# Batch 0's first attention in pieces, and batch 1's last values over another queue: an attention and feed-forward kernel on one Trainium2 core

## The chip, the core and the metric

The kernel runs on one core of one Trainium2 chip. The core has a matrix engine (TensorE, PE in the profile; PEld is its loading of weights), a vector engine (VectorE, DVE), an engine for activation functions (ScalarE, ACT), a general one (GpSimd, POOL) and one that mostly starts transfers (SyncE, SP). They run their own instruction streams in order and wait for each other by semaphores. Transfers (DMAs) are started from the queues of SP, ACT and POOL and share 16 DMA engines. PE writes its results to PSUM, the other data lies in SBUF.

The metric is the device time of the whole program in microseconds (us). Of the kernel before, three runs are given: 307.8, 309.38 and 309.56 us, median 309.38.

## The reference

There are 8 batches, 8 heads, 576 tokens and a head dimension of 64. Two attentions are added, and the sum goes through a feed-forward layer:

```python
q_d, k_d, v_d = means over 4 neighbouring tokens          # 144 tokens
out_d = softmax(q_d @ k_d.T / 8) @ v_d                    # "down"
out_up = repeat(out_d, 4)                                 # back to 576 tokens
mask = abs(pos[:, None] - pos[None, :]) < 4               # 7 neighbours
out_local = softmax(where(mask, q @ k.T / 8, -1e9)) @ v   # "local"
x = (out_up + out_local) as (8 * 576 tokens, 512)
h = x @ w_in                                              # 512 x 2048
out = (h * sigmoid(1.702 * h)) @ w_out                    # 2048 x 512
```

Inputs and outputs are 32-bit floats; the matmuls of the kernel take bf16.

## The kernel before, in words

All tokens together (4608) are worked through in 9 groups of 512. For a group `g`, `mm1` (L753) multiplies 16 chunks of `w_in` with the transposed attention result `xT` into PSUM (L738), ACT applies the activation (L749) into `gT`, and `mm2` (L770) multiplies with `w_out` (L808) and stores (`store`, L783). While group `g` is computed, the attention of batch `g + 1` is interleaved with its matmuls: the list `POS` or `POS_G` gives the places n (0 to 15 in `mm1`, 16 and up are the matmuls of `mm2`) at which the scores, the exponentials, the products with the values and the normalisations are issued. All engines follow an order that is written out by hand: each runs its instructions in program order.

Batch 0 has nothing to hide behind. It is done ahead of the loop, in the lines L847 to L938, and this is where most of the change lies. Its steps are these.

- **Loads.** `load_qk` (L192) and `load_vb` (L212) start transfers from POOL's queue that convert to bf16. A chunk of values `vb[:, i]`, i from 0 to 4, has 128 rows (two overlapping halves of 64 tokens) and comes in two transfers of 64 KB. Chunks 0 to 3 of batch 0 come this way; chunk 4 comes unconverted by `load_v` (L196), over SP's and ACT's queues, and ACT converts it (`prep_v`, L323). A transfer from POOL's queue waits until the eighth transfer before it has landed: they take turns on eight semaphores.
- **Scores.** `scores` and `scores_d` (L394, L411) give the local and the down scores of four heads, `exp_local` and `exp_down` (L477, L483) take their exponentials on ACT into `es` and `ed`.
- **Values of the down attention.** `prep_vd_pe` (L351) sums 4 neighbouring value rows by matmuls with the selection matrices `psel` (L362): part kc 0 needs chunks 0 and 1, kc 1 needs 1, 2 and 3, kc 2 needs 3 and 4. ACT copies the sums to `vd` (L371).
- **Products.** For a pair of heads `hp`, `av_local0` (L493, matmuls at L499) gives the local result into PSUM tile `o[hp]`, columns 0 to 259 from chunks 0 to 3 (two blocks of 65 columns from chunks 0 and 1, two from 2 and 3) and the rest from chunk 4; `av_down0` (L507, matmuls at L513 and L522) the down result. The tiles are `PA[0]`, `PA[1]`, `PA[2]` and `PA[0]` again for the four pairs; the scores use the same tiles before.
- **Norms.** `normalise0` (L537) divides by the sums on DVE: a reciprocal (L541), the product for the down part (L544) and for the local part (L549). Part "a" is columns 0 to 3 of seven, part "b" the rest.
- **Turning.** `turned` (L917) transposes and adds both results by matmuls with an identity (`transp_sum`, L564 and L575), and ACT copies them to `xT` (`copy_x`, L587 and L591).
- **First half of group 0.** `part` (L907) issues matmuls of `mm1` (L738) as soon as one pair's `xT` is there, in between the turning of the pairs.
- **Fillers.** `warm` (L603) issues matmuls on constants whose result nobody reads.

In the loop, for g = 0, POOL's queue starts the loads of batch 1's values, of `w_out` (four transfers of chunks 0 to 3, 4 to 7, 8 to 11, 12 and 13, 14 and 15; the first two are started ahead of the loop), and batch 2's q and k. `mm2` of group 0 takes chunks 0 to 7 of `w_out` first. At n = `VDP_0` batch 1's values are summed with `prep_vd_pe`; `by_head_dim` at places 42 and 56 gives batch 1's products and norms (`av_t`, L681, and `normalise_t`, L690 to L710).

Of the kernel before, what the change touches and what calls it, by code (L numbers as in the profile page):

```python
# [19 lines left out]
def kernel(  # L20
# [175 lines left out]
    def load_v(b, gate=None, chunks=range(5), queues=(nc.sync, nc.sync)):  # L196
        t = ldp.tile([128, 5, H, D], FP32, name="vf", tag="vf")
        vf[b] = t
        if gate is not None:
            gate(t[0:1, 0, 0, 0:1])  # L200
        for i in chunks:
            for par in range(2):
                queues[par].dma_start(
                    out=t[64 * par : 64 * par + 64, i],
                    in_=bass.AP(
                        tensor=v.tensor,
                        offset=v[b, 0].offset + (114 * i + KSTART[par]) * D,
                        ap=[[D, 64], [S * D, H], [1, D]],
                    ),
                )  # L210

    def load_vb(b, i):  # L212
        for par in range(2):
# [137 lines left out]
    def prep_vd_pe(b, pv, kcs=range(3), between=None):  # L351
        n = HP
        vb, vd = vbs[b % 2], vds[b % 2]
        for kc, iis in ((0, (0, 1)), (1, (1, 2, 3)), (2, (3, 4))):
            if kc not in kcs:
                continue
            c0 = 256 * (kc - kcs[0])
            if between and kc == 1:
                between()
            for i in iis:  # L360
                for j in range(2):
                    nc.tensor.matmul(  # L362
                        pv[64 * j : 64 * j + 64, c0 : c0 + D * n],
                        lhsT=psel[:, PSEL.index((i, kc)), :],
                        rhs=sub(
                            vb[:, i], 65 * (2 * j if b else j), (4 * 65, NQ), (65 * (1 if b else 2), 2), (1, D)
                        ),
                        start=(i == iis[0]), stop=(i == iis[-1]),
                        tile_position=(0, 64 * j),
                    )  # L370
        nc.scalar.copy(  # L371
            out=vd[:, kcs[0] : kcs[-1] + 1, :, 0:D],
            in_=pv[:, 0 : 256 * len(kcs)].rearrange(
                "p (k h d) -> p k h d", k=len(kcs), h=HP
            ),
        )
# [160 lines left out]
    def normalise0(o, y, u, parts="ab"):  # L537
        yl, yd, rc = y
        ov = o[:, :, 0:455].rearrange("p x (c e) -> p x c e", e=65)
        c0, c1 = {"a": (0, 4), "b": (4, 7), "ab": (0, 7)}[parts]  # L540
# [229 lines left out]
    def mm2(g, gT, steps):  # L770
# [29 lines left out]
        for t, ffc, run in order:  # L800
# [13 lines left out]
            if ffc == n_ffc - 1:  # L814
                store(t, ops[t], 0, d_model, nc.scalar, nc.sync, part.get(t))
# [23 lines left out]
    POS_G = {0: [16, 18, 29, 42, 56, 65], 1: [13, 16, 35, 44, 58, 65]}  # L839
    VDP_0 = 34  # L840
# [18 lines left out]
    warm(5, 256)  # L859
# [21 lines left out]
    load_w_out(4)  # L881
# [7 lines left out]
    warm(1, z=wf)  # L889
    prep_vd_pe(0, PM[0], range(0, 2))  # L890
    for hp in range(2):
        av_local0(hp, o[hp], range(5))
        normalise0(o[hp], y[hp], hp % 2, "a")
    prep_vd_pe(0, PM[1], range(2, 3))
    exp_down(1, scores_d(0, 1, PA[2]))
    nc.scalar.preload_act_table_set("silu_and_others")
    for hp in range(2):
        if hp == 1:
            warm(1, t=PM[0])
        av_down0(hp, o[hp])  # L900
        normalise0(o[hp], y[hp], hp % 2, "b")

# [9 lines left out]
    def av_whole0(hp):  # L912
        av_local0(hp, o[hp], range(5))
        av_down0(hp, o[hp])
        normalise0(o[hp], y[hp], hp % 2)

# [5 lines left out]
    av_whole0(2)  # L922
    warm(1, t=PM[0])
    turned(0, None)
    av_whole0(3)
# [14 lines left out]
    for g in range(n_groups):  # L940
        b = g + 1
        if g == 0:
            load_vb(1, 0)
# [6 lines left out]
            load_vb(1, 4)  # L950
# [57 lines left out]
        if b < B:  # L1008
# [3 lines left out]
            if g == 0:  # L1012
                steps.setdefault(VDP_0, []).append(lambda: prep_vd_pe(1, flat(PA[1])))
# [43 lines left out]
```

## Time and profile before

| what | value |
|---|---|
| median of the three runs shown | 309.38 us (307.8 to 309.56) |
| the profiled execution's own time | 308.58 us |
| its span, first to last instruction | 306.8 us, so 1.8 us lie around it |
| PE busy | 298.0 us, 97% of the span |
| ACT, DVE, POOL busy | 212.9, 187.1 and 178.9 us |
| PE busy between 0 and 13.5, 13.5 and 19, 19 and 24, 24 and 38.6 us | 10.56, 4.62, 3.56, 14.53 us |
| DMA traffic over the span | HBM read 44.83 MB, written 9.44 MB |

The profile shows one execution on the chip. Its page gives busy times, the chain of work that ended last and groups of instructions by line; the trace behind it can be asked for a timeline (instructions in order of time, merged where they are alike), for waits (who waited for whom) and for transfers. In a timeline a row has its start and length in us, then engine, line, operation, what it writes and reads, and in brackets the idle time ahead of it with what ended it. "issue" there is idle time that nothing in the profile explains. In the rows of DMA queues, q0 is POOL's, q1 SP's and ACT's, and the "instruction" queues bring the engines' own programs.

### The profile page before, as it was taken

To read this page: it belongs to the slowest core of one execution; us is meant where nothing else is said; L and a number is where in the kernel's file an instruction comes from. 1 tells how busy PE (TensorE), PEld (TensorE's weight loads), DVE (VectorE), ACT (ScalarE), POOL (GpSimd) and SP (SyncE) were. 2 spreads that over 40 slices of the span, in tenths; PEclk is the share of its full clock that TensorE was granted. 3 is DMA by queue.
4 is the path that set the end of the run, shared out by engine and by line. 5 is a ranking of instruction groups with operands and counts; after the bars stand their busy time and mean duration, and the time that the engine had idled before them with its cause. 6 is when DMAs were issued, how large, how long until landed. Compare 5 with 4: busy or idle time off the path is not lost.

```text
span 306.8 us, 8494 instructions
## 1 busy us (share of the span) xinstructions
PE 298.0 (97%) x3551; PEld 147.8 (48%) x3551; DVE 187.1 (61%) x354; ACT 212.9 (69%) x351; POOL 178.9 (58%) x217
## 2 busy tenths in 40 slices
PE   7879999999999999999999999999999999999995
PEld 3455455444554455445544554455444544444444
DVE  6865523966999689886897689777975430000000
ACT  5545887867887788668966896689769876226511
POOL 8855792599698968976797669845983300000000
PEclk9999999999999999999999999999999999999999
DMA  7999999999899969826973598425101110010012
GB/s 147 152 203 209 173 132 213 177 221 215 177 230 188 188 133 226 219 46 113 232 211 66 88 218 232 84 77 150 72 0 37 36 71 0 34 71 34 0 68 71
DMA packets 64662, 40.01 MB, mean 130 GB/s; under 512 B 44656, under 2 KB 56048, under 8 KB 64624
## 3 DMA queue, kind: packets, MB, share of 16 engines
q0 software_dynamic: 18352, 14.81, 35.8%
q1 hardware_dynamic: 45600, 24.46, 32.3%
q8 instruction: 28, 0.46, 0.6%
q10 hardware_dynamic: 672, 0.20, 0.3%
q14 instruction: 10, 0.08, 0.1%
HBM read 44.83 MB, written 9.44 MB: 177 GB/s over the span
## 4 chain that ended last, share of the span: by engine, by line
PE 93%; DMA 4%; issue 1%; POOL 1%; DVE 0%; ACT 0%; POOLq 0%; DVEq 0%
PE pm L808 40%; PE pm L738 36%; PE pa L681 5%; PE pa L738 5%; DMA qb<-in_q_dram 2%; DMA vb<-in_v_dram 2%; PE pa L449 2%; PE pm L824 1%; PE pa L458 1%; PE pa L394 1%; PE pa L411 0%; POOL kb L183 0%; PE pa L513 0%; PE pa L362 0%; PE pa L499 0%
## 5 line engine op out<-in xcount | busy, mean ns | idle before, releaser
L808 PE MATMUL pm<-w_out_bf,gT 128*128 128x512 bf16 x560 | 126.2, 379 | 0.0
L738 PE MATMUL pm<-xT,w_in_bf 128*128 128x512 bf16 x512 | 119.2, 379 | 0.3 <-ACT xT L591 0.3
L749 ACT ACTIVATE gT<-pm 128x512 bf16<-128x512 f32 x128 | 76.3, 598 | 42.7 <-PE pm L738 42.7
L738 PEld LDWEIGHTS <-w_in_bf 128*128 128x128 bf16 x576 | 55.6, 98 | 67.2 <-issue 0.6
L808 PEld LDWEIGHTS <-gT 128*128 128x128 bf16 x560 | 52.9, 98 | 62.2 <-issue 0.4
L699 DVE TENSOR_TENSOR xT<-pa,r 128x300 bf16<-128x300 f32 (+3 forms) x112 | 28.0, 303 | 18.6 <-ACT r L694 17.8
L787 ACT ACTIVATE osb<-pm 128x512 f32<-128x512 f32 (+2 forms) x37 | 21.5, 580 | 24.1 <-PE pm L808 21.3
L708 POOL TENSOR_TENSOR xT<-xT,ydt 128x576 bf16<-128x576 bf16 x14 | 16.2, 1173 | 31.1 <-DVE xT L699 31.1
L789 DVE TENSOR_SCALAR osb<-pm 128x128 f32<-128x128 f32 x1 | 0.3, 292 | 55.5 <-ACT osb L787 55.5
L491 DVE TENSOR_TENSOR es<-es,mask 128x600 bf16<-128x600 bf16 x28 | 19.0, 708 | 21.2 <-ACT es L477 20.9
L693 ACT ACTIVATE r<-pa 128x504 f32<-128x504 f32 (+1 forms) x42 | 24.0, 571 | 8.4 <-PE pa L681 8.4
L694 ACT ACTIVATE r<-r 128x504 f32<-128x504 f32 (+1 forms) x42 | 25.9, 616 | 1.3
L339 POOL TENSOR_TENSOR v<-v 112x512 f32<-112x512 f32 x18 | 23.5, 1306 | 0.4
L277 DVE TENSOR_REDUCE kT<-kT 32x576 bf16<-32x576 bf16 x22 | 17.5, 795 | 8.7 <-POOL odd L272 8.3
L261 DVE STREAM_TRANSPOSE kT<-kb 128x576 f32<-128x576 f32 x16 | 20.0, 1252 | 3.4 <-DMA kb<-in_k_dram 3.1
L477 ACT ACTIVATE es<-pa 128x600 bf16<-128x600 f32 x32 | 19.7, 668 | 3.4 <-PE pa L394 3.2
L261 DVE STREAM_TRANSPOSE qT<-qb 128x576 f32<-128x576 f32 x16 | 19.8, 1238 | 0.7 <-DMA qb<-in_q_dram 0.3
L738 PE MATMUL pa<-xT,w_in_bf 128*128 128x512 bf16 x64 | 20.0, 379 | 0.0
L315 POOL TENSOR_TENSOR pq<-qT 128x576 f32<-128x576 bf16 x14 | 16.0, 1145 | 6.8 <-DVE qT L277 6.6
L277 DVE TENSOR_REDUCE kT<-odd 32x576 bf16<-32x576 bf16 x22 | 17.5, 795 | 0.7
L277 DVE TENSOR_REDUCE qT<-qT 32x576 bf16<-32x576 bf16 x22 | 17.5, 795 | 0.7
L277 DVE TENSOR_REDUCE qT<-odd 32x576 bf16<-32x576 bf16 x22 | 17.4, 791 | 0.7
(107 smaller groups left out, 344.2 us busy)
## 6 DMA issues: line engine op xcount, KB each, us to landing
out_dram<-osb SPq DMA_DIRECT2D x35, 256.0 KB, 3.2
vf<-in_v_dram SPq DMA_DIRECT2D x61, 128.0 KB, 4.3
v<-in_v_dram SPq DMA_DIRECT2D x72, 96.0 KB, 4.2
kb<-in_k_dram POOLq DMA_DIRECT2D x16, 288.0 KB, 7.1
qb<-in_q_dram POOLq DMA_DIRECT2D x16, 288.0 KB, 9.4
w_in_bf<-in_moe_w_in_dram POOLq DMA_DIRECT2D x4, 512.0 KB, 7.5
w_out_bf<-in_moe_w_out_dram POOLq DMA_DIRECT2D x3, 512.0 KB, 15.6
vb<-in_v_dram POOLq DMA_DIRECT2D x18, 64.0 KB, 6.3
```

The lines of the kernel that those rows point to most:

```text
L261: nc.vector.transpose(out=t32.rearrange("p (i c) -> p c i", c=18), in_=store[b, qd].bitcast(FP32).rearrange("p (c d) -> p c d", c=18),)
L277: nc.vector.tensor_reduce(out=dst, in_=src[:, :, None], axis=mybir.AxisListType.X, op=ALU.add)
L339: eng.tensor_tensor(out=t1[0:112], in0=x[:, :, 0:2, :], in1=x[:, :, 2:4, :], op=ALU.add)
L477: nc.scalar.activation(out=es[2 * qd + u][:, :, 0:300], in_=sp[u][:, :, 0:300], func=AF.Exp, scale=inv_sqrt_d,)
L491: nc.vector.tensor_tensor(out=ev, in0=ev, in1=mask, op=ALU.mult)
L693: nc.scalar.activation(out=r, in_=den, func=AF.Ln)
L694: nc.scalar.activation(out=r, in_=r, func=AF.Exp, scale=-1.0)
L699: nc.vector.tensor_tensor(out=sub(x[u], t0 + at, (114, n), (1, c)), in0=sub(src, c0, (60, n), (1, c)), in1=sub(rc, c0, (60, n), (1, c)), o ...
L738: nc.tensor.matmul(acc, lhsT=w_in_bf[:, dmc, ffc * 128 : (ffc + 1) * 128], rhs=xT[dmc][:, g * TG : g * TG + TG], start=(dmc == 0), stop=(d ...
L749: nc.scalar.activation(out=gT[:, ffc, :], in_=acc, func=AF.Silu, scale=GELU_SCALE)
L787: eng.activation(out=osb, in_=ap, func=AF.Copy, scale=1.0 / GELU_SCALE)
L808: nc.tensor.matmul(ops[t], lhsT=gT[:, ffc, t * 128 : (t + 1) * 128], rhs=w_out_bf[:, ffc, :], start=(ffc % run == 0), stop=(ffc % run == r ...
```

## The change

- `prep_vd_pe` is split in `psum_v` (the sums of one part, by chunks, which may be left open for a later chunk) and `copy_vd`. For batch 1 the work is the same as before.
- For batch 0's pairs 0 and 1, the products are issued by chunk: chunks 0 and 1 first, with a norm of their two columns (part "p"); then the sums kc 0 with a copy of their own, and kc 1 as far as chunks 1 and 2; the second scores of the down attention; chunks 2 and 4; then chunk 3, with the norm of two more columns (part "q"), the rest of kc 1, and kc 2, both copied at once. The part "b" follows as before. Pair 2 is done right behind it, ahead of the turning of pair 0.
- Three fillers go (one of 512 columns of 32-bit floats ahead of the sums, two of 512 columns of bf16), and five fillers of 256 columns at the start become eight of 160.
- In POOL's queue the second transfer of `w_out` (chunks 4 to 7) goes behind the first of the two transfers of batch 1's chunk 0, in the loop.
- Batch 1's chunk 4 no longer comes converted over POOL's queue. It comes unconverted over SP's queue, behind a one-element memset on POOL that keeps its place in the order, and DVE converts it at n = 29.
- The places of batch 1's products move from 42 and 56 to 43 and 57, the sums of its values from 34 to 36. The store of group 0's first 128 tokens is scaled on DVE rather than ACT.

```diff
@@ -194,10 +194,11 @@
         load_1("q", q, qf, b, qd)
 
     def load_v(b, gate=None, chunks=range(5), queues=(nc.sync, nc.sync)):
+        c0 = chunks[0]
         t = ldp.tile([128, 5, H, D], FP32, name="vf", tag="vf")
         vf[b] = t
         if gate is not None:
-            gate(t[0:1, 0, 0, 0:1])
+            gate(t[0:1, c0, 0, 0:1])
         for i in chunks:
             for par in range(2):
                 queues[par].dma_start(
@@ -209,8 +210,8 @@
                     ),
                 )
 
-    def load_vb(b, i):
-        for par in range(2):
+    def load_vb(b, i, pars=range(2)):
+        for par in pars:
             nc.gpsimd.dma_start(
                 out=vbs[b % 2][64 * par : 64 * par + 64, i, :, 0:D],
                 in_=bass.AP(
@@ -348,32 +349,30 @@
     def flat(p):
         return p.rearrange("p x n -> p (x n)")
 
-    def prep_vd_pe(b, pv, kcs=range(3), between=None):
-        n = HP
-        vb, vd = vbs[b % 2], vds[b % 2]
+    def psum_v(b, kc, iis, p, ends=(True, True)):
+        vb = vbs[b % 2]
+        for i in iis:
+            for j in range(2):
+                nc.tensor.matmul(
+                    p[64 * j : 64 * j + 64],
+                    lhsT=psel[:, PSEL.index((i, kc)), :],
+                    rhs=sub(
+                        vb[:, i], 65 * (2 * j if b else j), (4 * 65, NQ), (65 * (1 if b else 2), 2), (1, D)
+                    ),
+                    start=(ends[0] and i == iis[0]), stop=(ends[1] and i == iis[-1]),
+                    tile_position=(0, 64 * j),
+                )
+
+    def copy_vd(b, kcs, pv):
+        nc.scalar.copy(
+            out=vds[b % 2][:, kcs[0] : kcs[-1] + 1, :, 0:D],
+            in_=pv.rearrange("p (k h d) -> p k h d", k=len(kcs), h=HP),
+        )
+
+    def prep_vd_pe(b, pv):
         for kc, iis in ((0, (0, 1)), (1, (1, 2, 3)), (2, (3, 4))):
-            if kc not in kcs:
-                continue
-            c0 = 256 * (kc - kcs[0])
-            if between and kc == 1:
-                between()
-            for i in iis:
-                for j in range(2):
-                    nc.tensor.matmul(
-                        pv[64 * j : 64 * j + 64, c0 : c0 + D * n],
-                        lhsT=psel[:, PSEL.index((i, kc)), :],
-                        rhs=sub(
-                            vb[:, i], 65 * (2 * j if b else j), (4 * 65, NQ), (65 * (1 if b else 2), 2), (1, D)
-                        ),
-                        start=(i == iis[0]), stop=(i == iis[-1]),
-                        tile_position=(0, 64 * j),
-                    )
-        nc.scalar.copy(
-            out=vd[:, kcs[0] : kcs[-1] + 1, :, 0:D],
-            in_=pv[:, 0 : 256 * len(kcs)].rearrange(
-                "p (k h d) -> p k h d", k=len(kcs), h=HP
-            ),
-        )
+            psum_v(b, kc, iis, pv[:, 256 * kc : 256 * kc + 256])
+        copy_vd(b, range(3), pv[:, 0:768])
 
 
     def bar_others(sp):
@@ -537,7 +536,7 @@
     def normalise0(o, y, u, parts="ab"):
         yl, yd, rc = y
         ov = o[:, :, 0:455].rearrange("p x (c e) -> p x c e", e=65)
-        c0, c1 = {"a": (0, 4), "b": (4, 7), "ab": (0, 7)}[parts]
+        c0, c1 = {"a": (0, 4), "b": (4, 7), "ab": (0, 7), "p": (0, 2), "q": (2, 4)}[parts]
         nc.vector.reciprocal(rc[:, :, c0:c1], ov[:, :, c0:c1, 64:65])
         if "b" in parts:
             st = 2 - u
@@ -812,7 +811,8 @@
                 start=(ffc % run == 0), stop=(ffc % run == run - 1),
             )
             if ffc == n_ffc - 1:
-                store(t, ops[t], 0, d_model, nc.scalar, nc.sync, part.get(t))
+                eng = nc.vector if (g, t) == (0, 0) else nc.scalar
+                store(t, ops[t], 0, d_model, eng, nc.sync, part.get(t))
             elif ffc % run == run - 1:
                 keep(t, ops[t])
 
@@ -836,8 +836,8 @@
             f()
 
     POS = [13, 16, 34, 44, 58, 65]
-    POS_G = {0: [16, 18, 29, 42, 56, 65], 1: [13, 16, 35, 44, 58, 65]}
-    VDP_0 = 34
+    POS_G = {0: [16, 18, 29, 43, 57, 65], 1: [13, 16, 35, 44, 58, 65]}
+    VDP_0 = 36
 
     o, y, x = {}, {}, {}
 
@@ -856,7 +856,7 @@
         load_vb(0, i)
     load_w_in(0, 512)
     warm(3, z=wf)
-    warm(5, 256)
+    warm(8, 160)
     make_off()
     make_ident(di)
     make_psel()
@@ -878,7 +878,6 @@
     for qd in range(NQ):
         load_qk(1, qd)
     load_w_out(0)
-    load_w_out(4)
     warm(2, z=wf)
     sp = scores(0, 1, PA[0:2])
     exp_local(1, sp)
@@ -886,19 +885,28 @@
     for hp in range(4):
         o[hp] = PA[hp % 3]
         y[hp] = y_tiles0()
-    warm(1, z=wf)
-    prep_vd_pe(0, PM[0], range(0, 2))
     for hp in range(2):
-        av_local0(hp, o[hp], range(5))
-        normalise0(o[hp], y[hp], hp % 2, "a")
-    prep_vd_pe(0, PM[1], range(2, 3))
+        av_local0(hp, o[hp], (0, 1))
+        normalise0(o[hp], y[hp], hp % 2, "p")
+    psum_v(0, 0, (0, 1), PM[1][:, 0:256])
+    copy_vd(0, (0,), PM[1][:, 0:256])
+    psum_v(0, 1, (1, 2), PM[0][:, 0:256], (True, False))
     exp_down(1, scores_d(0, 1, PA[2]))
+    for hp in range(2):
+        av_local0(hp, o[hp], (2, 4))
+    for hp in range(2):
+        av_local0(hp, o[hp], (3,))
+        normalise0(o[hp], y[hp], hp % 2, "q")
+    psum_v(0, 1, (3,), PM[0][:, 0:256], (False, True))
+    psum_v(0, 2, (3, 4), PM[0][:, 256:512])
+    copy_vd(0, (1, 2), PM[0])
     nc.scalar.preload_act_table_set("silu_and_others")
+    av_local0(2, o[2], range(5))
     for hp in range(2):
-        if hp == 1:
-            warm(1, t=PM[0])
         av_down0(hp, o[hp])
         normalise0(o[hp], y[hp], hp % 2, "b")
+    av_down0(2, o[2])
+    normalise0(o[2], y[2], 0)
 
     gT0 = new_gT()
     acc = PM + [PA[n][:, u, :] for n in (1, 2, 0) for u in range(2)]
@@ -909,20 +917,15 @@
             for ffc in ffcs:
                 hps_mm(0, ffc, dmc, acc[ffc])
 
-    def av_whole0(hp):
-        av_local0(hp, o[hp], range(5))
-        av_down0(hp, o[hp])
-        normalise0(o[hp], y[hp], hp % 2)
-
     def turned(hp, n):
         x = PM if n is None else [PA[n][:, u, :] for u in range(2)]
         transp_sum(y[hp], x)
         copy_x(0, hp, PM if n is None else PA[n][:, :, 0:288])
 
-    av_whole0(2)
-    warm(1, t=PM[0])
     turned(0, None)
-    av_whole0(3)
+    av_local0(3, o[3], range(5))
+    av_down0(3, o[3])
+    normalise0(o[3], y[3], 1)
     turned(1, 1)
     part((0, 1), 0)
     part((0, 1), 1)
@@ -940,14 +943,16 @@
     for g in range(n_groups):
         b = g + 1
         if g == 0:
-            load_vb(1, 0)
+            load_vb(1, 0, (0,))
+            load_w_out(4)
+            load_vb(1, 0, (1,))
             load_vb(1, 1)
             prep_qk(1, 0)
             pool_qk(1, 0)
             prep_qk(1, 1)
             load_vb(1, 2)
             load_vb(1, 3)
-            load_vb(1, 4)
+            load_v(1, gate=lambda t: nc.gpsimd.memset(t, 0.0), chunks=[4])
             load_w_out(8)
             load_w_out(12, 2)
             load_w_out(14, 2)
@@ -1010,6 +1015,7 @@
             for n, f in zip(pos, attention(b)):
                 steps.setdefault(n, []).append(f)
             if g == 0:
+                steps.setdefault(29, []).insert(0, lambda: prep_v(1, nc.vector, 4))
                 steps.setdefault(VDP_0, []).append(lambda: prep_vd_pe(1, flat(PA[1])))
             if g and b + 1 < B:
                 for n, f in (
```

## The prediction

> **What bounds the kernel now.** I read the page's busy times first (PE is busy for 97% of the span), then who waited for whom on PE over the whole span. This is the whole answer; its columns are the total wait, the number of waits and the longest.
>
> ```profile
> PE pm L606 <- DVE wf L111: 1.7, 1, 1.7
> PE pm L575 <- issue: 1.2, 1, 1.2
> PE pm L362 <- DMA vb<-in_v_dram: 0.8, 1, 0.8
> PE pa L394 <- DVE qT L261: 0.8, 1, 0.8
> PE pa L411 <- DVE qdT L304: 0.3, 1, 0.3
> PE pm L738 <- ACT xT L591: 0.3, 1, 0.3
> ```
>
> So PE never waits after the last of these, and in the timeline that one stands at 24.07 us. From there matmuls follow each other at 0.216 us (the eight of line 738 from 26.87 take 1.73 us) to the end. What the change can win is therefore the time by which this unbroken stream starts earlier, and what it can lose is a hole in it. Next I read PE's timeline ahead of that point:
>
> ```profile
> 14.51 0.75 PE L362 MATMUL pm<-vb,psel 128*64 128x256 bf16 x8
> 16.08 0.30 PE L362 MATMUL pm<-vb,psel 128*64 128x256 bf16 x2 [0.82 <-DMA vb<-in_v_dram]
> ...
> 19.99 0.41 PE L564 MATMUL pm<-id,yd 128*128 128x288 bf16 x3
> 20.23 0.29 PE L575 MATMUL pm<-id,yl 128*128 128x114 bf16 x3
> 21.75 0.33 PE L575 MATMUL pm<-id,yl 128*128 128x57 bf16 x5 [1.22 <-issue]
> ...
> 24.07 0.59 PE L738 MATMUL pm<-xT,w_in_bf 128*128 128x512 bf16 x2 [0.29 <-ACT xT L591]
> ```
>
> Two holes carry the argument. The first ends at 16.08 us, when the second half of value chunk 3 has landed (16.04 in the chain); all 40 products of pairs 0 and 1 (line 499) stand behind it, though only eight of them need this chunk. The second is the 1.43 us from 20.31, where the third matmul of line 575 starts, to 21.75, named "issue": a pause between alike matmuls of one `turned`, whose inputs were ready (the last norm of pair 0 ended at 19.48).
>
> **What the second hole is.** The transfers show it. The instruction queue q8 brings 28 packets, 0.46 MB, over the span: 16.4 KB each. PE has 3551 matmuls and 3551 weight loads, 254 for each packet, so one packet is a block of about 256 instructions for PE. Asked by windows, q8 moves one packet in each of 11.7 to 13.5, 19.4 to 20.4 and 25.5 to 26.6 us and none between; the line for 19.4 to 20.4 is
>
> ```profile
> q8 instruction: 1, 0.02, 5.6%
> ```
>
> 5.6% of 16 engines for 1 us is 0.9 us on one engine. Some 705 PE instructions are recorded ahead of the hole; a block boundary is at 768, and 63 set-up instructions that the records leave out would put it there. My reading is that PE ran out of instructions, and that the packet that ended at 20.38 let it go on at 21.75, 1.37 us later. A packet seems to be asked for when the block ahead of it is entered. With the same 63, instruction 512 ran at 16.35 us (in line 499's products), so asking to use took 5.4 us: 3.2 until the packet moved, 0.9 moving, 1.3 after. The neighbours give the bounds of this: the first packet, asked for near 9.2, moved from 11.7 and took 1.7; the third, asked for at 21.75, moved from 25.57. So asking to use may be 2.5 + 0.9 + 1.4 = 4.8 to 3.8 + 1.7 + 1.4 = 6.9 us.
>
> [...]
>
> **The new order, by its data.** Up to the down scores at 13.53 us little moves: eight fillers of 160 columns stream as many columns (1280) as five of 256 (0.71 us), and the score matmuls behind them wait for DVE (8.43) anyway. The filler at 13.46 (1.12 us) goes. Chunks 0 to 2 have landed by about 14.95, when line 362 goes on with chunk 2.
> - Ahead of chunk 3: 16 products, four sums of kc 0, four of kc 1, 24 down scores, 16 products. By the rows (40 products 0.57, eight sums 0.75, 24 scores 0.58) this is 0.23 + 0.75 + 0.58 + 0.23 = 1.8 us, from 13.6 (the tile `PA[0]` is free when ACT's exponentials have read it, 13.3; `PA[1]` at 13.93). It ends between 15.8 and, with a pause for the first packet (13.45 + 1.37 = 14.8 us; instruction 512 is now reached at about 14.05), 16.4. The norms "p" (a reciprocal of 0.2 and 256 columns at 0.41 each) lie on DVE, idle from 14.15 to 16.82.
> - Behind chunk 3, from 16.3: eight products 0.2, six sums 0.5, to 17.0; the copy of two parts 0.59 (line 371), to 17.6; `av_down0` 0.56, to 18.25; part "b" of pair 0 on DVE 0.98 (18.50 to 19.48 before), to 19.25. The norms "q" (2 x 0.65 from 16.45) end at 17.7, beside the copy. So `turned` can start its line 575 at 19.3 instead of 20.23, and is past the place of the pause at 19.45.
> - From the pause's end to the unbroken stream it was 24.07 - 21.75 = 2.32 us, the chain of turning, copying and the first `part`, which stays. Pair 2's norm, 1.5 us on DVE, would end at 21.65, ahead of its turning at 23.3. The fillers at 18.29 and 19.76 (0.32 each) go, and what was late behind them is DVE's part "b".
>
> By data alone the gain is 21.75 - 19.45 = 2.3 us.
>
> **The new order, by its instructions.** Up to this place the new PE program has six instructions more (three fillers at the start) and eight fewer (three fillers that go, the 32-bit one as two matmuls); products and sums are as many as before. So the boundary at 768 falls one matmul further in the same `turned`. Instruction 512 falls in the first 16 products, at 14.05, or at 14.8 if PE has to wait for the first packet. Its own packet is then usable 4.8 to 6.9 us later, 18.9 to 21.7; I take the 5.4 us of this very block and 14.8, so 20.2 us. The gain is 21.75 - 20.2 = 1.55, **1.5 us**, with 0 and 2.3 as its ends.
>
> **The rest of the change**, at nothing, with its cover:
> - `w_out` chunks 4 to 7: started at 23.41 instead of 20.54. It landed at 36.92 (16.4 us), behind full queues, and the 64 KB that now goes first landed 0.55 us after it, so it lands at about 37.5. `mm2` needs it four matmuls after 39.60, at 40.46, or 38.96 with my gain: 1.4 us of cover. If it landed 16.4 us after its start, 39.8, the gain is capped at 0.7.
> - Chunk 4 over SP: POOL saves two starts (0.7 each), SP waits for the memset, behind the start of chunk 3's second half; that waits for the eighth transfer before, now a value transfer that lands near 34.4 (33.85, the first `w_out`, + 0.55) instead of `w_out` at 36.9, so SP can start at 36; its queue is empty until 49. The nearest landing is 4.3 us (`vf`), so 41; in front of the sums at n = 36 (45.1 before, 43.6 now). DVE's cast is not in the trace; 0.3 (line 789, a quarter of it) to 0.7 us (line 549), in DVE's idle time between the masks (42.4 to 44.35). Queued behind it on DVE is the second mask, and behind that transfer's buffer batch 2's load, which POOL lets go at 49.06. If the chunk is late, PE waits at line 362 by as much as it passes 43.6.
> - The store on DVE, 0.3 to 0.7 us, falls where DVE waits for ACT (52.3 to 53.5), and ACT loses 0.6 there. If DVE were late, the next user of that PSUM tile, eight matmuls behind the second products, would wait. The moved places reorder PE's own work only.
>
> **The rivals.**
> 1. The pause does not return (the packet is there, or it was something else): 2.3 us, 306.3 of the profiled execution's 308.6. For it: the packet is asked for earlier. Against: 256 instructions then run in 5 us. 0.2.
> 2. The pause ends when it did, because transfers of `w_in` hold the packet up: gain 0 to 0.3, 308.4. For it: all DMA engines are busy from 14 us on (189 and 207 GB/s in the windows 13.5 to 19 and 19 to 24). 0.15.
> 3. `w_out` or the values are late as above: gain 0.7 or less, 307.9. 0.1.
> 4. Slower: without fillers PE's clock drops. At the start the 32-bit fillers are 0.853 us apart until 5.3 and 0.430 from 6.0 us, so 4.3 us of steady work at half speed; met again at the stream's start, this costs about 2.1 us, and the small matmuls ahead some 0.3 more. It decides when PE rests longer than the 1.43 us that did no harm; with the pause unchanged it gives 308.6 + 2.4 = 311, with the gain 309.5. The granted clock, 0.999, speaks against it. 0.07.
>
> [...]
>
> **How the numbers follow.** My forecast has 0.48. Against the profiled execution, 308.58 us, it gives 308.58 - 1.5 = 307.1; the median of the runs shown is 0.8 higher, so 307.9 by that; I take the middle, 307.5. The range takes rival 1 on a fast run with 0.9 us for the runs' own spread (306.3 - 0.9 = 305.4) and, at the top, rivals 2 and 3 on the median with some spread, to 309.9. Beyond are the fourth and mishaps. Faster by over 1% (below 306.3; 1% is about what a measurement of this kernel can tell from no change) needs rival 1 and luck, or a larger spread: 0.2. Slower by over 1% needs the fourth at its worst: 0.08. Within 1%: 0.72.
>
> **What the profile after would show.** A `turned` with "issue" ahead of its line 575 or 499 that ends near 20.2; the next q8 packet after the first near 18 us instead of 19.5; PE's last wait ending near 22.5; products of line 499 at 13.6 to 14; a wait of PE for chunk 3 at 16.1 shorter than 0.8 or none; `w_out`'s second start at 23.4, landing near 37.5, and no wait at line 808. Wrong would be: a pause that stays at 21.7, a new wait of line 362 at n = 36, or matmuls of line 738 more than 0.22 us apart.

## The result and the profile after

| | before | after |
|---|---|---|
| median | 309.12 us (20 executions, 307.8 to 314.62) | 310.75 us (20 executions, 308.65 to 312.13) |
| ratio to before, 95% interval | | 1.0044 [1.0025, 1.0064] |
| profiled execution, its span | 308.58, 306.8 us | 308.9, 307.1 us |

The changed kernel is 0.44% slower, about 1.4 us. (The ratios compare means of executions; one of before, 314.62 us, is left out, as it is over 1.5% above the fastest of that kernel, 307.8.) The forecast was 1.5 us faster; the median lies above the top of its range, 309.9. These are the head of the page of the kernel after, the clock in 40 slices, and who waited for whom on PE over the whole span (total wait, number, longest; the prediction opens with the same view of before).

```profile
span 307.1 us, 8499 instructions
...
PEclk9979999999999999999999999999999999999999
```

```profile
PE pa L393 <- DVE qT L262: 1.9, 2, 1.5
PE pm L605 <- DVE wf L111: 1.7, 1, 1.7
PE pa L498 <- issue: 0.7, 1, 0.7
PE pa L410 <- DVE qdT L305: 0.3, 1, 0.3
PE pm L737 <- ACT xT L590: 0.3, 1, 0.3
PE pa L498 <- ACT es L476: 0.3, 1, 0.3
PE pa L512 <- ACT vd L367: 0.2, 1, 0.2
```

The wait for value chunk 3 is gone and so is the wait of 1.2 us in the turning. The wait for batch 0's first q (line 393) is 1.1 us longer; that is a matter of when q landed, as said below. Two things are new: a wait named "issue" in the products (line 498), and the 7 in the third slice of the clock, 15.4 to 23.0 us. PE's timeline shows both (start, length, then the instruction):

```profile
14.49 0.26 PE L498 MATMUL pa<-vb,es 64*64 64x65 bf16 x8
15.01 0.25 PE L498 MATMUL pa<-vb,es 64*64 64x65 bf16 x5 [0.25 <-ACT es L476]
15.94 0.22 PE L498 MATMUL pa<-vb,es 64*64 64x65 bf16 x3 [0.68 <-issue]
16.09 0.99 PE L356 MATMUL pm<-vb,psel 128*64 128x256 bf16 x8
17.01 0.93 PE L410 MATMUL pa<-qdT,kdT 32*64 32x144 bf16 x24
...
21.67 0.60 PE L574 MATMUL pm<-id,yl 128*128 128x114 bf16 x8
...
24.27 0.59 PE L737 MATMUL pm<-xT,w_in_bf 128*128 128x512 bf16 x2 [0.29 <-ACT xT L590]
```

The eight sums of line 356 take 0.99 us (0.75 before) and the 24 scores of line 410 0.93 (0.58 before). The reason is the granted clock. Asked for stretches of 3.41 us, the columns are the stretch, its length, busy time and instructions of PE, PEld, DVE, ACT and POOL, then PE's clock, the DMA share and GB/s:

```profile
12.81:16.22 3.41, 2.13 (x122) 1.66 (x123) 2.89 (x4) 2.02 (x3) 3.26 (x5) 1.00 2.02 114
16.22:19.63 3.41, 3.41 (x84) 2.33 (x83) 1.57 (x6) 1.52 (x3) 3.41 (x7) 0.50 1.19 192
19.63:23.04 3.41, 3.18 (x93) 2.28 (x82) 2.54 (x10) 2.31 (x4) 0.67 (x1) 1.00 1.22 199
```

From 16.22 to 19.63 PE ran at half clock, behind a stretch in which it was busy for 62%. Of the 20 executions of the kernel after, 15 have a mean clock below 0.997; by their values (0.994 to 0.983, where one stretch of 3.41 us at half clock takes 0.0056 off the mean over 307 us) they hold one to three such stretches, an estimate. They average 310.78 us, the other five 309.50.

How fronts are compared: the first q of batch 0 lands at a different time in each profiled execution, 6.96 to 8.83 us, though the transfers ahead of it are the same in all kernels here. In before it landed at 7.10, here at 7.94. So the unbroken stream, at 24.27 instead of 24.07, starts 0.6 us earlier when counted from that landing, not 0.2 later. Counted so, this execution as a whole is 0.5 us shorter than the profiled one of before. The loss of 1.4 us is one of all executions together, and this profile does not hold it: one half-clock stretch alone, beside a gain at the front, does not make the kernel slower.

### The profile page after: what moved, and what is told of

Its sections match the earlier page's. It is cut to its first block, busy times and chain, and to the rows that moved or that the text cites. A ratio compares the mean times of both kernels' runs of the same rounds, so it can differ in the third digit from the quotient of the medians.

```text
span 307.1 us, 8499 instructions
## 1 busy us (share of the span) xinstructions
PE 298.3 (97%) x3550; PEld 148.6 (48%) x3550; DVE 189.6 (62%) x360; ACT 212.5 (69%) x350; POOL 177.7 (58%) x216
## 4 chain that ended last, share of the span: by engine, by line
PE 92%; DVE 2%; DMA 2%; ACT 2%; issue 1%; POOL 0%; POOLq 0%
PE pm L807 39%; PE pm L737 36%; PE pa L680 5%; PE pa L737 4%; DMA qb<-in_q_dram 2%; PE pa L448 2%; PE pm L824 1%; PE pa L393 1%; DVE qT L262 1%; PE pa L457 1%; PE pa L410 1%; PE pm L356 1%; PE pa L498 0%; ACT r L693 0%; ACT es L476 0%
## 5 line engine op out<-in xcount | busy, mean ns | idle before, releaser
L788 DVE TENSOR_SCALAR osb<-pm 128x512 f32<-128x512 f32 (+1 forms) x2 | 1.0, 486 | 55.5 <-ACT osb L786 55.5
```

## The experiments

Two theories stood after this profile. **A**: without the fillers PE's work is too thin somewhere, the clock drops, and that is the loss. **F**: PE is held by blocks of 256 instructions that arrive late, so a better order of the work only moves the pause. A third, **Q**, came with the second run: batch 1's chunk 4 is late over SP's queue and its cast on DVE. "Low clock" below counts executions with a mean clock under 0.997; the kernel before, run beside them, had 5 of 23, 7 of 29, 4 of 29 and 6 of 29 in the four groups.

### First group: fillers and places

**Before without the three fillers**, otherwise unchanged:

```diff
-    warm(1, z=wf)
     prep_vd_pe(0, PM[0], range(0, 2))
...
-        if hp == 1:
-            warm(1, t=PM[0])
         av_down0(hp, o[hp])
...
-    warm(1, t=PM[0])
     turned(0, None)
```

> The kernel before without the three fillers that the change takes out (one of 512 columns of 32-bit floats at 13.46 us, two of bf16 at 18.29 and 19.76); nothing else. Theory A, the clock: PE has too little work in one of the 3.4 us stretches between 12 and 23 us, and its granted clock falls to a half for the next. Then this kernel loses it too: mean granted clock 0.983 to 0.994 in most runs, 0.5 to 2 us slower than before. Theory B, the new order itself (or the queues) costs the time: the fillers are free, clock 0.999, within 0.3 us of before.

Measured: 313.11 us, ratio 1.0136 [1.0112, 1.0161], low clock in 6 of 6. By windows:

```profile
20.50:23.91 3.41, 1.64 (x46) 1.30 (x47) 2.03 (x6) 0.79 (x3) 0.83 (x2) 1.00 1.24 205
23.91:27.32 3.41, 3.25 (x18) 1.57 (x16) 0.81 (x1) 0.51 (x1) 1.30 (x2) 0.50 1.15 213
```

Three fillers whose results nobody reads, about 1.8 us of PE time, save 4 us. PE is busy for 48% in the stretch ahead of the drop (it holds the pause in the turning, here 2.0 us), and the dense matmuls of `mm1` that follow run at half speed. That the fillers hold the clock is shown. But the clock is not all of the 4 us: the mean clock of the six is 0.9895, that of before beside them 0.998, which is at most 2.6 us of a span of 308 (an estimate). In this profile the pause in the turning is 0.6 us longer than before's 1.4, and a new one of 0.7 us stands in batch 1's products, at 55.3 us.

**After with the 32-bit filler back**, ahead of the first products:

```diff
         y[hp] = y_tiles0()
+    warm(1, z=wf)
     for hp in range(2):
```

> The changed kernel with the 32-bit filler put back behind the first down scores, where PE waits for an instruction block (instruction 512, usable at 15.94 us in the profile after) and for the exponentials. Theory A: the clock holds (0.999 in most runs) and the kernel is 1 to 2 us faster than the changed one, so about as the kernel before, 0 to 0.7 us faster. Theory B: it stays 1 to 2 us slower than the kernel before, and the filler adds up to 0.3 us.

Measured: 310.17 us, 1.0036 [1.0007, 1.0065], low clock in 8 of 12. The profiled execution had full clock and the stream at 23.79, yet a span of 308.0 us: between 39.4 and 59.5, the start of `mm2` for group 0 and of `mm1` for group 1, it took 1.5 us more than before. One filler is too little for the clock, and there is a second loss, the wait of the sums for chunk 4:

```profile
PE pa L356 <- DVE vb L326: 1.1, 1, 1.1
```

**Before with 36 more PE instructions** (18 matmuls and their weight loads), the same columns of fillers:

```diff
-    warm(5, 256)
+    warm(23, 56)
```

> The kernel before with its five early fillers of 256 columns as 23 of 56 (1288 columns instead of 1280, 36 instructions more). Theory F, instruction blocks: the pause sits at the 705th recorded PE instruction whatever that is, so it moves 36 instructions ahead, out of the first turning into the products of pair 2 (line 522 or 513); instruction 512 is reached at 13.3 us, pauses there to about 14.4, its block's successor is usable near 19.8, and the stream starts 1 to 1.4 us earlier: 1 to 1.4 us faster. Theory G, the pause belongs to that matmul (its operands or its place in PSUM): the pause stays ahead of line 575 at 21.75 us, no change of the time.

Measured: 309.43 us, 1.0024 [0.9997, 1.0051], low clock in 6 of 12. The pause has left the turning and sits between two matmuls of the down scores:

```profile
13.57 0.57 PE L411 MATMUL pa<-qdT,kdT 32*64 32x144 bf16 x22 [0.31 <-DVE qdT L304]
15.42 0.25 PE L411 MATMUL pa<-qdT,kdT 32*64 32x144 bf16 x2 [1.28 <-issue]
```

The first row ends exactly with the 449th recorded PE instruction; in before the pause followed the 705th, 256 later, and the 705th is passed here without one. A pause that goes with the count of instructions and not with the matmul is a matter of the instructions, so the reading of F is shown. The 1 to 1.4 us expected were a miss: the pause came a block earlier instead, and the clock dropped more often than in before (behind a stretch, 12.90 to 16.31, in which PE was busy for 53%), though the fillers have as many columns.

**After without its queue part** (`w_out`, chunk 4, the store and the places as before):

```diff
+    load_w_out(4)
     warm(2, z=wf)
...
-            load_v(1, gate=lambda t: nc.gpsimd.memset(t, 0.0), chunks=[4])
+            load_vb(1, 4)
```

> The changed kernel with the front's new order alone: the loads of w_out and of batch 1's chunk 4, the places 42, 56 and 34 and the store on ACT as before. If the queue part costs or wins nothing, it is as the changed kernel, within 0.4 us (about 1.4 us over before, clock 0.983 to 0.999). If the moved transfers cost the time, it is 1 us or more faster than the changed kernel; if they earn some, slower, with a wait of PE for w_out or for the values in the loop.

Measured: 310.79 us, 1.0064 [1.0041, 1.0087], low clock in 5 of 6; a pause of 1.9 us at the 705th instruction and, by windows, a drop behind it:

```profile
18.69:22.10 3.41, 1.74 (x49) 1.36 (x50) 2.58 (x8) 0.80 (x2) 1.18 (x2) 1.00 1.23 202
22.10:25.51 3.41, 3.41 (x20) 1.56 (x17) 1.29 (x2) 0.64 (x1) 0.70 (x1) 0.50 1.20 212
```

So the pieces without fillers lose by themselves. One more pause, of 1.0 us, stands at 145.5, at the 4033rd recorded instruction (14 blocks of 256 behind the 449th). The interval overlaps that of the whole change; what the queue part costs inside it can't be read from this run.

### Second group: the parts by themselves

**Pieces with three fillers, transfers as before.** To the kernel of the run before this one are added:

```diff
+    warm(1, z=wf)
     for hp in range(2):
...
     av_local0(2, o[2], range(5))
+    warm(1, t=PM[1])
...
     normalise0(o[2], y[2], 0)
+    warm(1, t=PM[0])
```

> The changed kernel's order of the front alone (transfers, places and store as before), with three fillers in the new order: the 32-bit one behind the first down scores, one of bf16 ahead of av_down0 of pair 0, one ahead of the first turning. Theory A (clock) with F (instruction blocks): the clock holds in most runs, the pause at the 705th recorded instruction stays (it ends 5.4 to 6.5 us after the 449th), and the whole is within 0.7 us of before, 1.5 us or more faster than the same order without fillers (310.8). Theory B (the new order costs time in itself): it stays 1.5 us slower than before.

Measured: 309.42 us, 1.0022 [0.9994, 1.0051], low clock in 2 of 12 instead of 5 of 6. The fillers hold the clock in most executions. The order still wins nothing: its timeline has a pause at the 449th instruction and another at the 705th, and the stream starts at 25.25, 17.3 us after q's landing, against 17.0 in before.

```profile
16.22 0.25 PE L498 MATMUL pa<-vb,es 64*64 64x65 bf16 x5 [0.56 <-issue]
...
22.80 0.46 PE L574 MATMUL pm<-id,yl 128*128 128x114 bf16 x8 [1.52 <-issue]
```

**Before with the queue part alone**, the rest of which (`load_v`, `load_vb`, the store, the places) is as in the change's diff:

```diff
-    load_w_out(4)
...
-            load_vb(1, 0)
+            load_vb(1, 0, (0,))
+            load_w_out(4)
+            load_vb(1, 0, (1,))
...
-            load_vb(1, 4)
+            load_v(1, gate=lambda t: nc.gpsimd.memset(t, 0.0), chunks=[4])
...
+                steps.setdefault(29, []).insert(0, lambda: prep_v(1, nc.vector, 4))
```

> The kernel before with the queue part alone: w_out chunks 4 to 7 behind the first transfer of batch 1's values, chunk 4 over SP's queue with the cast on DVE, the places 43, 57 and 36, the store on DVE. Theory Q: the values land near 44 us over SP instead of 42.2 over POOL, and the cast, which ran for 2.14 us beside POOL's memset of v4 and 0.49 without, is late for the sums at n = 36; PE waits up to 1.1 us at line 362, 0.5 to 1.3 us slower than before with the clock at 0.999. If the queue part is free: within 0.3 us of before.

Measured: 309.68 us, 1.0036 [1.0009, 1.0062], low clock in 1 of 12. So the queue part loses by itself, with the clock held. The rows of DVE and of POOL around the cast:

```profile
43.73 2.65 POOL L961 MEMSET v<- 32x3072 f32 x1
44.45 2.22 DVE L326 CAST vb<-vf 128x512 bf16<-128x512 f32 x1 [1.54 <-DMA vf<-in_v_dram]
46.59 0.83 DVE L492 TENSOR_TENSOR es<-es,mask 128x600 bf16<-128x600 bf16 x2
```

The cast takes 2.22 us and ends 0.29 us after POOL's memset of `v4`, at whose start it had not yet begun. In the filler run above it took 2.14 and also ended 0.29 after the memset. In before POOL's memset had run beside the second pair of DVE's mask products (line 491, two inputs), and these took as long as the first pair, which ran alone:

```profile
41.34 1.03 DVE L491 TENSOR_TENSOR es<-es,mask 128x600 bf16<-128x600 bf16 x2 [5.83 <-ACT es L477]
44.35 1.03 DVE L491 TENSOR_TENSOR es<-es,mask 128x600 bf16<-128x600 bf16 x2 [1.98 <-ACT es L477]
```

```profile
43.62 2.65 POOL L958 MEMSET v<- 32x3072 f32 x1
```

In the profile of the kernel after the cast came first, and took 0.49:

```profile
44.30 0.49 DVE L326 CAST vb<-vf 128x512 bf16<-128x512 f32 x1 [1.73 <-DMA vf<-in_v_dram]
```

```profile
44.58 2.81 POOL L963 MEMSET v<- 32x3072 f32 x1
```

But PE's waits in the loop show that the long cast is the smaller part of this profile's loss:

```profile
PE pa L682 <- issue: 1.3, 1, 1.3
...
PE pa L363 <- DVE vb L326: 0.2, 1, 0.2
```

The 1.3 us stand at 54.9, in batch 1's products (line 682), at the 1723rd recorded instruction; six matmul records are missing ahead of it, so it is the 1729th, a block boundary again. The same pause stood in before without fillers (0.7 us at 55.3), whose queues are before's, and is not in the profile of before. So the queue part's 0.36% are measured, but how they divide between the cast and a late block is not shown.

**After with one filler and the memset moved** up to the loads of batch 1, ahead of the cast:

```diff
             load_v(1, gate=lambda t: nc.gpsimd.memset(t, 0.0), chunks=[4])
+            nc.gpsimd.memset(v4[32:64], 0.0)
             load_w_out(8)
...
                 load_qk(2, qd)
-            nc.gpsimd.memset(v4[32:64], 0.0)
```

> The changed kernel with the 32-bit filler (as the earlier run with it, 310.17 us) and POOL's memset of v4 moved ahead, right behind the one-element memset, where POOL waits for w_out anyway (37.1 to 39.5 us). Theory Q with the collision: the cast takes 0.5 us whatever the run, PE waits less than 0.4 us ahead of the sums, and the kernel is 0.5 to 1 us faster than the earlier run. If the cast was slow for another reason, it stays 2.1 us long and the time as it was.

Measured: 310.73 us, 1.0059 [1.0032, 1.0086], low clock in 8 of 12. The expected gain of 0.5 to 1 us over the run with one filler (310.17 us, in another group) is a miss. The cast is short again, and PE no longer waits for it, but a pause of 1.0 us now stands at the 1729th instruction (53.9 us):

```profile
43.72 0.43 DVE L326 CAST vb<-vf 128x512 bf16<-128x512 f32 x1 [1.22 <-DMA vf<-in_v_dram]
```

With one filler the clock still drops in most executions; the four at full clock average 309.24 us, the others 311.09.

**Before with POOL held by two memsets** (5.3 us; the one of the loop goes) ahead of the second to fourth transfers of `w_in`:

```diff
     reduce_qk(0, 1, "k")
+    for r in (32, 64):
+        nc.gpsimd.memset(v4[r : r + 32], 0.0)
     for c in range(1, 4):
```

> The kernel before with POOL held for some 5 us (the memset of v4 and a second one like it) ahead of w_in chunks 4 to 15, so that fewer transfers are under way when PE asks for its third block at 16.3 us. Theory F: the packet moves within 1 to 2 us of being asked for instead of 3.1, and the pause at the 705th recorded instruction shrinks to less than 0.5 us; the stream starts near 23 us. What follows is late (batch 1's q and k, w_out), so PE waits in the loop and the whole is not faster. If the pause is no fetch or the packet is slow whatever else moves: the pause stays 1.2 to 1.5 us.

Measured, in two executions alone: 313.45 us, 1.0156 [1.0111, 1.0202]. No transfer moves from 17.2 to 20.7 us (0 GB/s in all 16 slices), the pause in the turning is gone (20.07 to 20.12 at the 705th instruction) and the stream starts at 22.44 though q landed 0.9 later than in before. The time is lost again in the loop, where PE waits for `w_out` and for the pooled q of batch 1:

```profile
PE pm L808 <- DMA w_out_bf<-in_moe_w_out_dram: 2.9, 2, 2.3
...
PE pa L411 <- POOL qdT L319: 1.1, 1, 1.1
```

### Third group: all fillers, and a shorter hold

**After with all three fillers**, at the places shown above.

> The whole change with three fillers put back (as in the run of the pieces with three fillers; here with the changed transfers, places and store). Theory A: the share of runs whose mean granted clock is below 0.997 falls from 14 in 20 to about that of before, and the kernel is 0.3% or more faster than without fillers against before: ratio 1.000 to 1.003. If the queue part costs what it cost alone on the kernel before (0.36%), the ratio is 1.003 to 1.006 with the clock held; if it is hidden here, 1.000 to 1.002.

Measured: 309.63 us, 1.0027 [0.9996, 1.0057], low clock in 3 of 12. This profiled execution, at full clock and with q at 6.96, is the nearest to that of before. The pause is back in the turning, and the stream starts at 23.38:

```profile
20.92 0.46 PE L574 MATMUL pm<-id,yl 128*128 128x114 bf16 x8 [1.23 <-issue]
...
23.38 0.59 PE L737 MATMUL pm<-xT,w_in_bf 128*128 128x512 bf16 x2 [0.29 <-ACT xT L590]
```

Counted from q's landing that is 16.42 us, against 16.97 in before: this front is 0.55 us shorter. But that is one pair of executions: in the profile of the run with the memset moved as well (fourth group), whose front is the same, it took 17.3. Behind it the cast met the memset (42.99 to 45.64), and the stretch from `mm2`'s start for group 0 to `mm1`'s for group 1 grew from 18.55 to 19.66 us, more than the front had won; PE waited 0.7 us of it for the cast:

```profile
43.08 2.85 DVE L326 CAST vb<-vf 128x512 bf16<-128x512 f32 x1 [1.40 <-DMA vf<-in_v_dram]
```

```profile
PE pa L356 <- DVE vb L326: 0.7, 1, 0.7
```

**Before with one memset** (2.65 us, moved from the loop) as the hold, and batch 1's products and sums at the later places 43, 57 and 36:

```diff
     reduce_qk(0, 1, "k")
+    nc.gpsimd.memset(v4[32:64], 0.0)
     for c in range(1, 4):
```

> The kernel before with one memset of v4 (2.65 us) moved from the loop to ahead of w_in chunks 4 to 15 on POOL, and the places 43, 57 and 36. Theory F: as with two memsets, PE's third block comes through a lighter load, so the pause at the 705th recorded instruction is below 0.5 us instead of 1.4 and the stream starts 1 us or more earlier against the landing of batch 0's q; the later transfers are only some 2 us late, which w_out (38.9 against a need at 39.1) and the values (44 against 43.7) just bear. 0.5 to 1.2 us faster than before, ratio 0.996 to 0.998. If the late transfers eat it: ratio 0.998 to 1.003 with a wait of PE for w_out or at line 362.

Measured: 310.75 us, 1.0055 [1.003, 1.008], low clock in 1 of 12. The 705th instruction is passed without a pause (20.67 to 20.68). The shares of the DMA engines from 15 to 19.5 us, in 40 slices, first in before:

```profile
DMA  9999999999999999999999999999999999999999
```

and with the hold:

```profile
DMA  9999999999999994115101001010000022990085
```

In before PE entered the block ahead of the pause at 16.35, and the next packet moved from 19.48; here the block is entered at 16.71 and the packet moves from 17.11. By this pair of profiles, what holds it up is the traffic. But the traffic is needed: `w_out`'s second transfer now lands at 40.84 (36.92 in before). PE waits 1.3 us for it, and 1.7 for a later one at 53.6:

```profile
PE pm L808 <- DMA w_out_bf<-in_moe_w_out_dram: 3.0, 2, 1.7
```

**The pieces with three fillers and this hold** (the two edits together, transfers otherwise as before):

> The pieces with three fillers (ratio 1.0022, 0.9994 to 1.0051), and the memset and places as in the run before this one. With the third block early, the new order is no longer held up by it: if its data order is worth what the prediction made of it (0.8 us of the 2.3), this is the fastest, ratio 0.993 to 0.997. If the second block, at the 449th recorded instruction, holds the pieces up (0.76 us there in their profile), it is as the kernel before with the memset moved, 0.997 to 1.000.

Measured: 310.98 us, 1.0063 [1.0037, 1.0088], low clock in 1 of 12. No pause, `w_out` at 42.02, PE waits 2.8 us for `w_out`. A miss for the hope that the order becomes worth something once the pause is gone.

### Fourth group

**After with three fillers and the memset moved**, the mends for A and Q together:

> The whole change with three fillers (ratio 1.0027, 0.9996 to 1.0057; in its profile the cast took 2.85 us and PE waited 0.7 us for it) and POOL's memset of v4 moved ahead of the cast. If the queue part's loss is the cast beside the memset: the cast takes 0.4 to 0.5 us, PE doesn't wait ahead of the sums, and the kernel gains some 1 us: ratio 0.997 to 1.000, clock held in most runs. If the late landing over SP is the loss, whatever the cast takes: ratio 1.002 to 1.004 with a wait at line 356.

Measured: 309.52 us, 1.0006 [0.9973, 1.0039], low clock in 4 of 12. The cast took 0.42 us, and PE did not wait for it; a pause of 0.7 us stands at the 1729th instruction (55.4 us). This is as fast as before and no more. Its eight executions at full clock average 308.69 us, those of before in the same group 308.91; with the memset in its place they averaged 309.59 (nine executions), beside 309.08 for before. With one filler the same step went from 309.94 (before 308.77) to 309.24 (before 308.59), four executions each. Against before that is 0.7 and 0.5 us better with the memset moved. It fits a loss by the long cast, but the executions are few and the intervals of the whole runs overlap, so it is not shown.

**A hold of 1.8 us**, two thirds of the memset, in before and in the pieces with fillers:

```diff
+    nc.gpsimd.memset(v4[32:64, 0:2], 0.0)
     for c in range(1, 4):
...
-            nc.gpsimd.memset(v4[32:64], 0.0)
+            nc.gpsimd.memset(v4[32:64, 2:3], 0.0)
```

> The kernel before with two thirds of the memset of v4 (1.8 us) ahead of w_in chunks 4 to 15 and the rest where it was. The hold of 2.65 us took the pause at the 705th recorded instruction away, and made w_out 3.9 us late (40.84 us) with PE waiting 3.0 us for it. Theory F: a shorter hold lets the transfers behind it keep their time within 1 us (w_out by 38) and the packet still finds a lighter load, so the pause is 0.3 to 1 us instead of 1.4: 0.3 to 0.8 us faster than before, ratio 0.997 to 0.999. If the load is as heavy by 16.3 us whenever the transfers are issued before that: pause as before, ratio 0.999 to 1.002.

> The pieces with three fillers and transfers as before (ratio 1.0022), with the same shorter hold. As the run before this one by theory F, with the new order's gain of the front (0.4 us or so against the landing of batch 0's q) on top: ratio 0.995 to 0.999. If the second block (instruction 449) is the limit: 0.999 to 1.002.

Measured: 310.1 us, 1.0036 [1.0005, 1.0068], and 310.29 us, 1.0046 [1.0018, 1.0074], low clock in 1 of 12 each. The one profile of the first ran at a mean clock of 0.95 and is not used. In the second the pause at the 705th instruction is gone (21.36 to 21.39), one of 1.1 us is left at the 449th, and PE waits 1.1 us for `w_out`. By the medians the hold costs less the shorter it is, and none of the three lengths won anything, against what was expected of each of the shorter ones.

No kernel tried is faster than before.

## Why the prediction was wrong, by its steps

- **"Without fillers PE's clock drops", rival 4, was put at 0.07, and is what happened.** The step that failed is the point from which it decides, a rest "longer than the 1.43 us that did no harm". In the kernel after the longest single rest from 12.8 us on is 0.9 us, and the clock dropped all the same. In its place the traces show stretches of 3.41 us: the half-clock stretches in the work shown above are all that long, and in after the one in the work and one at the very end start 85 times 3.413 us apart (16.22 and 306.35). Counted on this grid, drops came behind stretches with PE busy for 0.62 (after), 0.53, 0.51, 0.48, 0.48, 0.47 and 0.32 of the time. A thin stretch is not enough, though: with 0.48 (39.64 to 43.05 in the pieces with the hold of 2.65 us), 0.50 (37.26 to 40.67 in before with two memsets) and 0.55 (from 5.98 in after) none followed. Before has 0.68, 0.98 and 0.64 from 12.65 on, and its clock held in that execution. "The granted clock, 0.999, speaks against it" was read from one execution: in a fifth of its executions (22 of 110) the kernel before drops as well, so it stood near the edge. The price was set too high: forecast 2.1 to 2.4 us, measured 1.3 between executions of the kernel after with and without a drop. With the shares (15 of 20 against a fifth) that is some 0.7 us of the 1.4, an estimate. The other half remains at full clock: in such executions the kernel after averages 309.50, before 308.6 to 309.1 in its four groups.
- **"What the second hole is" was right**, a block of 256 instructions: the pause went with the count. In the front it stood at recorded instruction 449 or 705 in every kernel that had one, and in the loop at the 1729th in four profiles (0.7 to 1.3 us, 53.9 to 55.4) and at the 4033rd in one. So the rows have pauses of 0.7 to 2.0 us at counts that are whole blocks of 256 apart; the prediction looked for them in the front alone.
- **"Usable 4.8 to 6.9 us later ... I take the 5.4 us" is the term of the front's sum that was mis-sized.** The start of block 512, 14.8, was nearly right: 15.94 in after, with q 0.84 late, and 14.63 with three fillers, with q 0.14 early. But from there to the use of the next block it took 6.0 us (to 21.96) and 6.3 (to 20.92). The packet forecast near 18 moved from 19.61 in after, 3.7 us after the block ahead of it was entered. I had treated the 5.4 us as a delay of the fetch itself; with the `w_in` transfers held back in before, the packet moved 0.4 us after the block ahead of it was entered (one memset, 16.71 to 17.11) instead of 3.1. That is rival 2's reason, "transfers of `w_in` hold the packet up", though it had only 0.15. Of the 1.5 us the front kept 0.55 to 0.64 in these two profiles; in the others with the pieces and no hold it was between 0.3 us lost and 1.2 won, so the figure is no more than a pair of executions.
- **"By data alone"** held: products start 6.55 us after q's landing (13.6 forecast, 6.5 after q), and the wait for chunk 3 is gone. With POOL held the pieces reach the stream 14.9 us after q's landing, where the forecast's 2.3 us mean 14.7. But the old order, with the same hold, reaches it after 15.4: by this pair of executions, of those 2.3 us some 0.5 belong to the order and the rest to the pause, whose removal PE pays back waiting for `w_out`.
- **"The rest of the change, at nothing" failed for chunk 4.** It was to land at 41; SP could start its two halves only at 38.14 and 38.80 and they landed at 43.72 and 44.18, with the DMA engines busy (the DMA share is 90% or more in 35 of 40 slices from 38.14 to 44.18, 60% or more in the rest). The cast, "0.3 to 0.7", took 0.42 to 0.49 alone but 2.14 to 2.85 when POOL's memset had begun first. That memset stood in the trace of before at 43.62, 2.65 us long, in the very place to which I moved the cast; I looked for DVE's idle time and not for POOL's row. PE's sums waited 0.2 to 1.1 us for the long cast. The part alone costs 0.36%, with the share of the cast open. When the memset had begun first, the cast ended 0.29 us after it each time; the mask products, which have two inputs, took 1.03 us alone and beside the memset. Why the one is held up and the other is not, no run shows.
- **`w_out`**'s second transfer (of five) started at 25.56 instead of 23.4 and landed at 39.9 instead of 37.5; PE did not wait for it in after, whose `mm2` started at 39.80. The store on DVE cost nothing that a wait shows.

What stays open: which of the three fillers matters most (one was too few, three enough); what beside PE's busy share decides that a thin stretch drops the clock; why q's landing varies by 1.9 us; why the block at the 1729th instruction came late in some kernels only; and how the 1.4 us divide between the clock, the cast and late blocks, since the intervals of the runs overlap.

## What to carry to other kernels

A filler that sits in a stretch where PE is busy for only half to two thirds of the time is not idle decoration (here the clock dropped behind stretches with PE busy for 0.32 to 0.62): before removing one, add up PE's busy time in the windows of 3.4 us that the traces of this case showed, and look at the clock of several executions, not of one. The pauses of 0.7 to 2.0 us named "issue" here stood at whole blocks of 256 PE instructions. The one of before fell elsewhere when instructions were added ahead of it (from the 705th to the 449th), and in another run it was gone when, with the traffic held back, the next packet moved 0.4 us after the block ahead of it was entered instead of 3.1, so a gain "up to the pause" must be priced by the DMA load. When an operation is moved into another engine's idle time, look also at what POOL does at that moment: here a cast of 0.42 to 0.49 us became one of 2.14 to 2.85.

## What the runs showed of the hardware that was not expected

- A cast of 128x512 from 32 to 16 bits on DVE that starts while a memset on POOL runs ends 0.29 us after it, in three profiles of three: 0.42 to 0.49 us becomes 2.14 to 2.85. One that began first delays the memset little (2.81 instead of 2.65 us). Mask products of 128x600 in 16 bits are not slowed (1.03 us for two, alone and beside the memset).
- Half clock for 3.41 us after a stretch with PE busy for 0.62, although no single rest in it was longer than 0.9 us; and none after another with 0.48 (39.64 to 43.05 in the pieces with the hold of 2.65 us).
- An instruction packet of 16.4 KB moved 3.1 us after the block ahead of it was entered while the DMA share was 90% or more in 39 of 40 slices (before, 16.3 to 20.4 us), and 0.4 us after with the traffic held back by 2.65 us.
